# Ones rows, v cast and row halves placed anew at the start of an attention and feed-forward kernel

## The chip, the cores and the metric

The kernel runs on one NeuronCore of a Trainium2 chip. The metric is the device time of one execution in microseconds. The core has TensorE (PE, with PEld for its weight loads), VectorE (DVE), ScalarE (ACT), GpSimd (POOL) and SyncE (SP), which here only issues DMAs. Each engine works through its own queue in order.

## The reference

Attention with a mask from hash buckets (4 batches, 8 heads, 768 positions, head size 64), then a feed-forward layer of 2048 on the 3072 rows of 512:

```python
q_bucket = sum((q @ proj > 0) * 2 ** arange(6))       # k_bucket likewise
scores = where(q_bucket == k_bucket, q @ k.T / 8, -1e9)
attn = softmax(scores)                                # minus the row maximum
x = (attn @ v) as 3072 x 512
h = x @ w_in
g = where(h >= 1, h, where(h <= -1, 0, (h + 1) ** 2 / 4))
out = g @ w_out
```

## The kernel before

The 32 heads go two by two, as 16 pairs. Every fp32 operand is split into a high part that TensorE takes and a low rest. For a pair, T2 holds the high parts with some extra rows and T1 the low ones. Rows 0 to 7 of T2 carry the hash bits, scaled so that unequal buckets push the score far down. For the first pair the row maximum is in row 32 of T2[0]: in `T2[0][32:33, 0, h]` lies the clamped maximum of each query (the max row), and in `T2[0][32:33, 1, h]` lie ones that it is multiplied with (the ones row). For later pairs the max row is row 7.

A head is cut into 12 units (NU) of 128 keys by 384 queries. In the main loop step g does, on TensorE, the score matmuls of unit g (`s_unit`, lines 350 and 351), the three value matmuls of unit g - 4 (`pv_unit`, lines 383 to 385), and in some steps one of the six pairs of maxima matmuls of a later head (`max_mm`, line 310), whose result VectorE reduces in the next step (`max_red`, line 314). All maxima share one PSUM tile, `smax`. ScalarE takes the exponential twice for each unit, VectorE or POOL subtracts to get the low part (`lo_unit`, line 39; POOL for units 0 and 3 of each six). Other work is put into steps by `at(g, function, ...)`; within a step it is recorded behind the unit's own work, in the order of the calls. `early` says in which steps the maxima of heads 0 to 4 lie; from then on every second step has one.

Ahead of the loop the first pair is prepared by hand. `prep_first(0)` on VectorE and `prep_first(1)` on POOL split the raw tiles, `place_first` issues DMAs that put rows in place, `first_mm` computes the projections, `first_cmp` and `first_scale` make bits of them, and `max_first` computes the maxima of the first three query blocks of head 0 in six matmuls with a filler each (`keep_busy`, line 402). The other three blocks of head 0 come in steps 0 to 2, those of head 1 in steps 3 to 8. `row_clamp` clamps maxima into a helper tile, `row_mm` transposes them by small matmuls (line 254), and ScalarE copies the row into T2[0] (`row_half`, `row_both`). `quarter` splits a quarter of the second pair, `move` copies parts between T1 and T2, `bits_mm`, `bits_cmp`, `bits_scale` and `bits_put` make the bits rows of a later pair, `load_v`, `cast_v` and `split_v` bring v, `weights_pair` makes the split projection for two heads.

The order on each engine is that of the recorded calls. What an instruction waits for follows from the tiles that it reads and writes: a matmul that reads rows 0 to 127 of `T2[0][:, 1, h]` waits for the last recorded write to any of these rows.

Of the kernel before, what the change touches and what calls it, by code (L numbers as in the profile page):

```python
# [11 lines left out]
F32 = mybir.dt.float32  # L12
# [9 lines left out]
NB = 6  # L22
# [91 lines left out]
def attention(ctx, tc, wst, T1, T2, qk, v, pj, cv, x_d, s_d, e_d, tasks, shared):  # L114
# [16 lines left out]
    nrow = [const.tile([P, NJ, 33], F32R, name=f"nrow{h}") for h in range(2)]  # L131
    pj_raw = const.tile([P, NB], F32, name="pj_raw")
    pj_hi = const.tile([P, NB], F32R, name="pj_hi")
    pw = const.tile([P, 3, P], F32R, name="pw")
# [8 lines left out]
    def load_raw(pr):  # L143
        raws[pr] = work.tile([P, 2, S], F32, name="raw", bufs=1)
        nc.sync.dma_start(out=raws[pr], in_=qk[pr])

# [10 lines left out]
    def move(pr, part):  # L157
        t1, t2 = T1[pr % NQK].bitcast(F32), T2[pr % NQK].bitcast(F32)
        src, dst = ((t2[0:64, 1], t2[64:128, 0]), (t2[64:128, 1], t1[0:64, 1]),
                    (t1[64:128, 0], t1[64:128, 1]), (t2[0:64, 1], t1[64:128, 0]))[part]  # L160
        nc.sync.dma_start(out=dst, in_=src)
# [4 lines left out]
    def prep_first(h, raw, eng):  # L166
# [16 lines left out]
        if h == 1:  # L183
            for sl in halves:
                low(sl)

    def place_first(h):
# [60 lines left out]
    def row_flags(hd):  # L248
        nc.vector.tensor_scalar(out=nms[hd][:, NJ:2 * NJ], in0=nms[hd][:, 0:NJ], scalar1=CLAMP, scalar2=None,
                                op0=ALU.is_gt)  # L250
# [5 lines left out]

    def row_both(hd):
        ps = ps_m.tile([P, 2, 512], F32, name="smax")
        for hf in range(2):
            row_mm(hd, hf, ps[:, hf])  # L260
        nc.scalar.copy(out=T2[0][32:33, 0, hd, :].rearrange("p (f n) -> p f n", f=2), in_=ps[32:33, :, 0:HS])

    def row_half(hd, hf):
        ps = obank[hf]
        row_mm(hd, hf, ps)
        nc.scalar.copy(out=T2[0][32:33, 0, hd, hf * HS:(hf + 1) * HS], in_=ps[32:33, 0:HS])
# [49 lines left out]

    mx = {}

    def max_clamp(hd, eng):
# [79 lines left out]

    def keep_busy():  # L400

        nc.tensor.matmul(out=scratch[:, 0:2 * P], lhsT=idle[:, 0:P], rhs=idle, start=True, stop=True)

    def weights_pair(part):

        if part == 0:
            nc.scalar.copy(out=pj_hi, in_=pj_raw)
        for i, r, c in ((0, 0, 0), (0, 64, 16), (1, 0, 8), (1, 64, 24)):
            rows = slice(r, r + 64)
            if part == 0:  # L410
                nc.scalar.copy(out=pw[rows, i, c:c + NB], in_=pj_hi[rows].bitcast(F32))
            else:
                sub(nc, nc.gpsimd, pw[rows, i, 32 + c:32 + c + NB], pj_raw[rows], pj_hi[rows].bitcast(F32))
# [35 lines left out]
    nc.vector.memset(T2[0][0:64, 0].bitcast(F32), 0.0)  # L449
    for _ in range(12):  # L450
        keep_busy()
# [6 lines left out]
    for t in PH:  # L458
        nc.gpsimd.memset(t[:, HS:HS + 2].bitcast(F32), 1.0)
    for r, c in ((0, 0), (64, 32)):  # L460
        nc.scalar.copy(out=pw[r:r + 64, 2, c:c + NB], in_=pj_raw[r:r + 64])
    prep_first(0, first[0][:, 0], nc.vector)
    place_first(0)
    load_raw(1)
    load_v(0)
    for hf in range(2):
        first_mm(0, hf, obank[hf])
    nc.gpsimd.memset(T2[0][32:33, 1, 0].bitcast(F32), 1.0)
    for _ in range(5):
# [13 lines left out]
    for hf in range(2):  # L483
        first_mm(1, hf, ps_s.tile([P, 512], F32, name="s"))
    row_half(0, 0)
    for hf in range(2):
        first_cmp(1, hf)
    for _ in range(4):
        keep_busy()
    for t in VB:  # L490
        nc.gpsimd.memset(t[:, :, 1].bitcast(F32), 0.0)
    for t in PL:
        nc.gpsimd.memset(t[:, HS:HS + 2].bitcast(F32), 0.0)

    def quarter(n):
# [7 lines left out]

    quarter(0)
    quarter(1)
    at(0, first_scale, 1, 1, nc.vector)
    at(1, cast_v, 0, nc.vector)
    for h in range(2):
        at(1, split_v, 0, nc.gpsimd, h)
    at(1, weights_pair, 0)  # L510
    at(2, first_scale, 1, 0, nc.vector)
    at(9, lambda: nc.vector.memset(T2[0][32:33, 1, 1].bitcast(F32), 1.0))
    for n in (2, 3):
        at(n, quarter, n)
    at(2, weights_pair, 1)
    at(10, load_v, 1)
    at(3, row_clamp, 0, NJ // 2, NJ)
    at(5, load_raw, 2)
    at(4, row_half, 0, 1)
    for n in range(3):  # L520
        at(4, move, 1, n)
    for hf, n in enumerate((5, 7)):
        at(n, bits_mm, 1, hf, 1)
        at(n + 1, bits_cmp, 1, hf)
    at(5, row_flags, 0)
    at(6, lambda: nc.gpsimd.memset(T2[1][0:64, 0].bitcast(F32), 0.0))
    at(11, max_tr, 0, 0)
    at(11, max_put, 0)
    at(9, row_clamp, 1, 0, NJ)
    at(8, move, 1, 3)  # L530
    at(8, bits_scale, 1, nc.scalar)
    at(9, bits_put, 1)
    at(10, row_both, 1)
    at(11, row_flags, 1)
    at(12, lambda: nc.gpsimd.memset(T2[2][0:64, 0].bitcast(F32), 0.0))
    at(15, max_tr, 1, 0)
    at(15, max_put, 1)
    at(2 * NU + 1, lambda: nc.gpsimd.memset(T2[0][32:33, 0].bitcast(F32), 0.0))
    for hd in range(NH):
        pr, h = hd // 2, hd % 2  # L540
        g = hd * NU
        if hd + 2 < NH:
            gc, gt = ((NU + 8, NU + 8), (2 * NU + 4, 2 * NU + 6))[hd] if hd < 2 else (g + NU, g + NU + 4)
            at(gc, max_clamp, hd + 2, nc.gpsimd if hd > 1 else nc.vector)
            at(gt, max_tr, hd + 2, 1)
            at(gt + (hd > 1), max_put, hd + 2)
        if h == 0 and pr + 2 < NPAIR:
            g0 = g + (9 if pr == 0 else 0)
            for n in range(4):
# [5 lines left out]
            if pr + 3 < NPAIR:  # L555
                at(g0 + 7, load_raw, pr + 3)
            bits_at = ((7, 1), (11, 0)) if pr else ((13, 0), (17, 1))
            for hf, (n, bank) in enumerate(bits_at):
# [3 lines left out]
            at(g + n + 2, bits_scale, pr + 2, nc.gpsimd)  # L562
            at(g + (18 if pr else 21), bits_put, pr + 2)
        if h == 0 and pr + 1 < NPAIR:
            gv = g + LAG + (2 if pr else 10)
            at(gv, cast_v, pr + 1, nc.scalar)
            at(gv + 1, split_v, pr + 1, nc.gpsimd, 0)
            at(gv + 3, split_v, pr + 1, nc.gpsimd, 1)
            if pr + 2 < NPAIR:
                at(gv + 6, load_v, pr + 2)  # L570

    NG = NH * NU
    red = None
    early = {n: (0, NJ // 2 + n) for n in range(NJ // 2)}
    for hd, gs in ((1, range(3, 9)), (2, range(14, 20)), (3, (20, 21, 23, 24, 26, 27)),
                   (4, (28, 29, 31, 32, 34, 35))):
        early.update({n: (hd, i) for i, n in enumerate(gs)})
    for g in range(NG + LAG + 1):
# [5 lines left out]
        if 1 <= g <= NG:  # L584
            lo_unit(g - 1)
        if g < 3 * NU:
            due = g in early
            hd, i = early.get(g, (0, 0))
        else:
            hd, i = g // NU + 2, (g % NU) // 2  # L590
            due = hd < NH and g % 2 == 0
# [661 lines left out]
```

## Time and profile before

| | us |
|---|---|
| median of 3 runs | 985.62 (983.16 to 987.43) |
| the profiled execution | 986.29 |
| its span | 984.5 |
| PE busy | 968.2 |
| DVE busy | 799.5 |
| ACT busy | 679.3 |
| POOL busy | 342.1 |

The span is what the trace covers; the execution's own time is 1.8 us longer. Granted clock means TensorE's clock as a share of full speed; its mean over the span was 0.996. In the views, a row of the timeline is start, duration, engine, line, operation, output and input, with the idle time just before it and what ended it in brackets.

### The profile page before, as it was taken

The page shows a single profiled execution, that of the slowest core. Times are in us where ns is not written, and L with a number is a line of the kernel's source. Part 1 is how long each engine was busy: PE and PEld are TensorE (multiplying, and loading weights), DVE is VectorE, ACT ScalarE, POOL GpSimd, SP SyncE. Part 2 cuts the span into 40 slices and gives each one's busy share as a digit, 9 for nine tenths or more (in the row PEclk, how much of TensorE's full clock was granted, in tenths as well). Part 3 has the DMA queues.
Part 4 walks back from the last instruction along what each step waited for, and adds up shares of the span by engine and source line. Part 5 has one row for each costly group of instructions (what it writes and reads, how often), then busy time and mean ns, then how long its engine had stood idle before and what let it go on. Part 6 is the DMA issues. An engine that isn't in the chain of part 4 may idle for free.

```text
span 984.5 us, 15564 instructions
## 1 busy us (share of the span) xinstructions
PE 968.2 (98%) x5047; PEld 891.9 (91%) x5047; DVE 799.5 (81%) x1359; ACT 679.3 (69%) x1483; POOL 342.1 (35%) x411
## 2 busy tenths in 40 slices
PE   7999999999999999999999999999999999999998
PEld 5789999999999999999999998888988888988896
DVE  8789999999999999988798887887876777655554
ACT  6779888998999888988655556555564545554444
POOL 7666777778877777766100000000000000000000
PEclk8999999999999999999999999999999999999999
DMA  6654667766656667554496478977449554454431
GB/s 174 177 154 101 174 179 191 199 173 168 177 140 180 173 187 191 136 146 124 127 286 217 118 245 271 299 239 210 118 151 245 147 185 116 130 168 118 115 93 64
DMA packets 94712, 167.55 MB, mean 170 GB/s; under 512 B 13940, under 2 KB 51432, under 8 KB 94632
## 3 DMA queue, kind: packets, MB, share of 16 engines
q1 hardware_dynamic: 94408, 166.56, 59.3%
q8 instruction: 40, 0.66, 0.3%
q14 instruction: 40, 0.33, 0.1%
q10 hardware_dynamic: 224, 0.00, 0.0%
HBM read 106.13 MB, written 33.87 MB: 142 GB/s over the span
## 4 chain that ended last, share of the span: by engine, by line
PE 90%; DVE 5%; ACT 2%; DMA 1%; issue 1%; SPq 0%; DVEq 0%
PE y L791 27%; PE h L1023 18%; PE smax L310 7%; PE h L928 7%; PE o L385 6%; PE s L351 6%; PE o L384 6%; PE o L383 6%; PE s L350 6%; PE o L204 2%; DVE nm L314 2%; DMA vraw<-in_v_dram 1%; DVE pl L39 1%; DMA t<-te 1%; ACT ph L359 0%
## 5 line engine op out<-in xcount | busy, mean ns | idle before, releaser
L359 ACT ACTIVATE ph<-s 128x384 fp32r<-128x384 f32 x380 | 188.1, 495 | 47.5 <-PE s L351 41.8
L314 DVE TENSOR_REDUCE nm<-smax 128x1 f32<-128x768 f32 x189 | 178.9, 947 | 16.2 <-PE smax L310 14.5
L39 POOL TENSOR_TENSOR pl<-pf,ph 128x384 fp32r<-128x384 f32 x128 | 139.0, 1089 | 90.4 <-ACT pf L364 90.1
L756 DVE SCALAR_TENSOR_TENSOR t<-t 128x384 f32<-128x384 f32 x128 | 71.3, 557 | 101.7 <-ACT z L751 101.5
L39 DVE TENSOR_TENSOR pl<-s,ph 128x384 fp32r<-128x384 f32 x256 | 135.5, 544 | 10.2 <-ACT s L364 9.4
L350 PE MATMUL s<-t 128*128 128x384 f32 x384 | 132.6, 345 | 0.0
L385 PE MATMUL o<-pl,va 128*128 128x386 f32 x384 | 130.6, 340 | 0.4 <-DVE pl L39 0.4
L384 PE MATMUL o<-ph,vb 128*128 128x386 f32 x384 | 130.6, 340 | 0.0
L351 PE MATMUL s<-t 128*128 128x384 f32 x384 | 130.3, 339 | 0.2 <-DMA t<-te 0.2
L383 PE MATMUL o<-ph,va 128*128 128x386 f32 x384 | 130.2, 339 | 0.1
L364 ACT ACTIVATE s<-s 128x384 f32<-128x384 f32 x252 | 124.9, 496 | 0.0
L791 PE MATMUL y<-t,ghi 128*128 128x512 f32 x384 | 124.6, 395 | 0.0
L310 PE MATMUL smax<-t 128*128 128x384 f32 x378 | 104.0, 356 | 6.6 <-DVE nm L314 6.1
L750 ACT ACTIVATE t<-h,mh 128x384 f32<-128x384 f32 x56 | 32.6, 581 | 84.4 <-PE h L928 44.3
L310 PEld LDWEIGHTS smax<-t 128*128 128x128 f32 x378 | 65.5, 191 | 23.5 <-DVE nm L314 23.0
L761 ACT CAST ghi<-z 128x384 fp32r<-128x384 f32 x129 | 65.1, 505 | 30.1 <-DVE z L757 26.3
L751 ACT ACTIVATE z<-t,m 128x384 f32<-128x384 f32 x128 | 79.0, 617 | 4.2
L1023 PE MATMUL h<-wbig,t 128*128 128x384 f32 x399 | 81.4, 336 | 0.0
L791 PEld LDWEIGHTS y<-t,ghi 128*128 128x128 f32 x384 | 71.3, 188 | 11.1 <-ACT ghi L761 0.3
L1023 PEld LDWEIGHTS h<-wbig,t 128*128 128x128 f32 x399 | 71.6, 188 | 5.3
L791 PE MATMUL y<-t,glo 128*128 128x512 f32 x192 | 76.0, 396 | 0.0
L791 PE MATMUL y<-woh,glo 128*128 128x512 f32 x192 | 75.7, 394 | 0.2
(181 smaller groups left out, 2092.0 us busy)
## 6 DMA issues: line engine op xcount, KB each, us to landing
t<-wc SPq DMA_DIRECT2D x92, 256.0 KB
t<-t SPq DMA_DIRECT2D x60, 384.0 KB
wraw<-wc SPq DMA_DIRECT2D x76, 256.0 KB
raw<-in_qk_dram SPq DMA_DIRECT2D x15, 768.0 KB
wraw<-in_w_in_dram SPq DMA_DIRECT2D x16, 512.0 KB
wraw<-in_w_out_dram SPq DMA_DIRECT2D x16, 512.0 KB
t<-ed SPq DMA_DIRECT2D x36, 192.0 KB
xd<-xs SPq DMA_DIRECT2D x32, 192.5 KB
```

The source lines that it names most:

```text
L39: eng.tensor_tensor(out=out, in0=a, in1=b, op=ALU.subtract)
L310: nc.tensor.matmul(out=smax[hd][:, hf, 0:HS], lhsT=t2[:, 0, h, i * P:(i + 1) * P], rhs=t2[:, 1, h, hf * HS:(hf + 1) * HS], start=True, sto ...
L314: nc.vector.tensor_reduce(out=nmp(hd)[:, i:i + 1], in_=smax[hd][:, :, 0:HS], axis=AX.XY, op=ALU.max, negate=True)
L350: nc.tensor.matmul(out=ps[:, 0:HS], lhsT=t1[:, 1, h, ks], rhs=t1[:, 0, h, sl], start=True, stop=False)
L351: nc.tensor.matmul(out=ps[:, 0:HS], lhsT=t2[:, 1, h, ks], rhs=t2[:, 0, h, sl], start=False, stop=True)
L359: nc.scalar.activation(out=ph[:, 0:HS], in_=ps[:, 0:HS], func=AF.Exp, scale=SCALE)
L364: nc.scalar.activation(out=pf, in_=ps[:, 0:HS], func=AF.Exp, scale=SCALE)
L383: nc.tensor.matmul(out=o, lhsT=wa, rhs=ph, start=(jj == 0), stop=False)
L384: nc.tensor.matmul(out=o, lhsT=wb, rhs=ph, start=False, stop=False)
L385: nc.tensor.matmul(out=o, lhsT=wa, rhs=pl, start=False, stop=(jj == NJ - 1))
L791: nc.tensor.matmul(out=ys[c][m], lhsT=g_[:, m * P:(m + 1) * P], rhs=w, start=(first and k == 0), stop=(last and k == 2))
L1023: nc.tensor.matmul(out=ps, lhsT=w[:, cs], rhs=x, start=(n == 0 and s not in (2, 3, 6)), stop=(n == 5), skip_group_check=True)
```

## The change

- v of the first pair is loaded ahead of the second pair's raw tile, which comes in two halves. The v cast goes from VectorE to POOL, ahead of the loop, with the split of its first head; the split of the second head is put in step 10.
- The pair weights are made on POOL, before and inside the second head's preparation. The first head's ones row is set behind that on POOL, the second head's in step 2 on POOL (before: step 9 on VectorE).
- `first_scale` of the second head and `row_flags` go to POOL.
- The fourth pair of maxima of head 0 comes ahead of the loop, the others in steps 0 and 2, those of head 1 in steps 4 to 12.
- The second head's max row is set in two halves, steps 7 to 9 and 13 to 14. The third head's maxima are clamped, transposed and put in two halves, steps 18 to 25.
- The quarters, moves, bits and v of the second and third pair are put in other steps; the raw load of the third pair goes out ahead of the bits rows and of later moves.
- From head 5 on, maxima lie two steps later, their clamps one.
- Two more fillers at the start; the four behind the first row write into another bank.

```diff
 def load_raw(pr):
-        nc.sync.dma_start(out=raws[pr], in_=qk[pr])
+        for sl in (slice(0, HS), slice(HS, S)) if pr == 1 else (slice(0, S),):
+            nc.sync.dma_start(out=raws[pr][:, :, sl], in_=qk[pr][:, :, sl])
...
 (prep_first, h == 1)
                 low(sl)
+            weights_pair(1)
+            ones_row(0)
+
+    def ones_row(h):
+        nc.gpsimd.memset(T2[0][32:33, 1, h].bitcast(F32), 1.0)
...
+    def half_clamp(hd, hf):
+        nm = nms[hd]
+        x = nm[:, hf * HB:(hf + 1) * HB]
+        nc.vector.tensor_scalar(out=nmh[:, hf, HB:2 * HB], in0=x, scalar1=CLAMP, scalar2=None, op0=ALU.is_gt)
+        nc.vector.tensor_scalar(out=nmh[:, hf, 0:HB], in0=x, scalar1=CLAMP, scalar2=None, op0=ALU.min)
+
+    def half_put(hd, hf, bank):
...
+        nc.tensor.transpose(out=ps[0:2 * HB, 0:P], in_=nmh[:, hf], identity=ident)
+        te = small.tile([2 * NJ, P], F32R, name="te")[0:2 * HB]
+        nc.scalar.copy(out=te, in_=ps[0:2 * HB, 0:P])
...
-    for _ in range(12):
+    for _ in range(14):
         keep_busy()
...
+    weights_pair(0)
...
-    load_raw(1)
     load_v(0)
+    load_raw(1)
...
-    nc.gpsimd.memset(T2[0][32:33, 1, 0].bitcast(F32), 1.0)
...
-    row_half(0, 0)
+    for n in (0, 1):
+        max_mm(0, NJ + n)
+    row_half(0, 0, 0)
+    max_red(0, NJ // 2)
     for hf in range(2):
         first_cmp(1, hf)
     for _ in range(4):
-        keep_busy()
+        keep_busy(obank[1])
+    cast_v(0, nc.gpsimd)
...
+    split_v(0, nc.gpsimd, 0)
...
-    quarter(0)
-    quarter(1)
-    at(0, first_scale, 1, 1, nc.vector)
-    at(1, cast_v, 0, nc.vector)
...
-    at(9, lambda: nc.vector.memset(T2[0][32:33, 1, 1].bitcast(F32), 1.0))
...
-    at(5, load_raw, 2)
...
+    for t in (1, 0):
+        at(0, first_scale, 1, t, nc.gpsimd)
+    at(2, ones_row, 1)
     at(3, row_clamp, 0, NJ // 2, NJ)
+    at(4, row_half, 0, 1, 1)
+    for n, g in enumerate((1, 4, 5, 6)):
+        at(g, quarter, n)
...
+    at(7, row_clamp, 1, 0, NJ // 2)
...
+    at(9, row_half, 1, 0)
...
+    at(10, load_raw, 2)
...
+    at(13, row_clamp, 1, NJ // 2, NJ)
+    at(14, row_half, 1, 1, 0)
...
-    early = {n: (0, NJ // 2 + n) for n in range(NJ // 2)}
-    for hd, gs in ((1, range(3, 9)), (2, range(14, 20)), (3, (20, 21, 23, 24, 26, 27)),
-                   (4, (28, 29, 31, 32, 34, 35))):
+    early = {}
+    for hd, gs in ((0, (0, 2)), (1, (4, 5, 6, 8, 11, 12)), (2, (15, 16, 17, 19, 20, 22)),
+                   (3, (21, 23, 24, 26, 27, 29)), (4, (30, 31, 33, 34, 36, 37))):
...
-            hd, i = g // NU + 2, (g % NU) // 2
+            hd, i = (g - 2) // NU + 2, (g - 2) % NU // 2
```

How the rows move on the engines. First POOL's queue from its last memset of the tiles ph on, before the loop; t_0_77 is T2[0], t_2_76 the first pair's low rest, raw tiles of the first pair are wraw. Before:

```order
L459 MEMSET ph_160 128x2
L468 MEMSET t_0_77 1x768
L175 CAST t_0_77<-wraw 128x384 x2
L39 TENSOR_TENSOR t_2_76<-wraw,t_0_77 128x384 x2
L491 MEMSET vb_152 128x6x64
```

After:

```order
L481 MEMSET ph_161 128x2
L429 CAST pj_hi<-pj_raw 128x6
L433 CAST pw<-pj_hi 64x6 x4
L177 CAST t_0_77<-wraw 128x384 x2
L39 TENSOR_TENSOR t_2_76<-wraw,t_0_77 128x384 x2
L39 TENSOR_TENSOR pw<-pj_raw,pj_hi 64x6 x4
L192 MEMSET t_0_77 1x768
L290 CAST va_151<-vraw 128x6x2x64
```

The memset of the first head's ones row (1x768) went from the first place to behind the weights and the second head's preparation.

Then the same queue in the loop's first steps, from the last memset of the tiles pl on; t_1_78 and t_1_75 are T2 and T1 of the second pair, pl low parts of the units, vb the low part of v. Before:

```order
L493 MEMSET pl_167 128x2
L150 CAST t_1_78<-raw 128x384
L39 TENSOR_TENSOR t_1_75<-raw,t_1_78 128x384
L39 TENSOR_TENSOR pl_161<-pf,ph_154 128x384
L39 TENSOR_TENSOR vb_152<-vraw,va_150 128x6x64 x2
```

After:

```order
L519 MEMSET pl_168 128x2
L39 TENSOR_TENSOR vb_153<-vraw,va_151 128x6x64
L248 TENSOR_SCALAR t_0_77<-xs,cvd 8x768 x2
L39 TENSOR_TENSOR pl_162<-pf,ph_155 128x384
L152 CAST t_1_78<-raw 128x384
L39 TENSOR_TENSOR t_1_75<-raw,t_1_78 128x384
L192 MEMSET t_0_77 1x768
```

The second head's bits (L248) and its ones row (the last memset) are now in this queue, with one low part and one quarter between them.

Last TensorE, from the first score matmuls to the first maxima of the second head; s are scores, smax maxima, o the value sums. Before:

```order
L350 MATMUL s<-t_0_74 128x384
L351 MATMUL s<-t_0_77 128x384
L310 MATMUL smax<-t_0_77 128x384 x2
L350 MATMUL s<-t_0_74 128x384
L351 MATMUL s<-t_0_77 128x384
L310 MATMUL smax<-t_0_77 128x384 x2
L350 MATMUL s<-t_0_74 128x384
L351 MATMUL s<-t_0_77 128x384
L310 MATMUL smax<-t_0_77 128x384 x2
L350 MATMUL s<-t_0_74 128x384
L351 MATMUL s<-t_0_77 128x384
L310 MATMUL smax<-t_0_77 128x384 x2
```

After, the last rows ahead of the second head's first maxima, from step 3 on:

```order
L372 MATMUL s<-t_0_74 128x384
L373 MATMUL s<-t_0_77 128x384
L372 MATMUL s<-t_0_74 128x384
L373 MATMUL s<-t_0_77 128x384
L405 MATMUL o_137<-ph_156,va_151 128x386
L406 MATMUL o_137<-ph_156,vb_153 128x386
L407 MATMUL o_137<-pl_163,va_151 128x386
L311 MATMUL smax<-t_0_77 128x384 x2
L261 MATMUL o_138<-ident_r,nrow_145 33x128 x3
```

The second head's first maxima came in step 3 right behind those of the first head; now they come in step 4 behind five score units and the first value unit, and read the ones row that POOL sets.

98 lines of the change are left out of this document (50 added, 48 removed).

## The prediction

> **What bounds the kernel now.** I read the page first, then stage windows, then the waits of the engine that is busiest, then its neighbours at the places where it waits.
>
> ```profile
> span 984.5 us, 15564 instructions
> PE 90%; DVE 5%; ACT 2%; DMA 1%; issue 1%; SPq 0%; DVEq 0%
> ```
>
> The profiled execution took 986.29 us, 1.8 us more than its span; the three timed runs have a median of 985.62, so 0.67 us less. All sums below start from 986.29. TensorE carries 90% of the chain that ended last, so the question is where TensorE stands still or runs slowly. The windows (busy us with counts for PE, PEld, DVE, ACT, POOL, then granted clock, DMA share, GB/s) answer that:
>
> ```profile
> 5.00:6.30 1.30, 1.15 (x8) 0.85 (x7) 1.00 (x3) 0.87 (x2) 0.73 (x1) 1.00 0.03 9
> 14.80:18.20 3.40, 1.01 (x5) 0.65 (x4) 2.92 (x5) 2.08 (x7) 3.32 (x5) 0.99 0.47 123
> 18.20:21.60 3.40, 2.60 (x8) 2.60 (x9) 2.69 (x4) 1.72 (x5) 3.21 (x6) 0.50 0.42 89
> 21.60:25.00 3.40, 3.40 (x14) 3.25 (x13) 2.71 (x4) 1.34 (x3) 3.30 (x4) 0.50 0.85 202
> 25.00:38.40 13.40, 11.88 (x70) 11.19 (x70) 10.13 (x17) 10.37 (x24) 8.39 (x11) 1.00 0.54 142
> 38.40:80.00 41.60, 39.54 (x212) 35.79 (x212) 33.61 (x51) 31.27 (x75) 25.61 (x29) 1.00 0.61 163
> 80.00:600.00 520.00, 518.49 (x2812) 489.98 (x2811) 476.62 (x748) 425.10 (x983) 289.71 (x325) 1.00 0.62 174
> 600.00:984.50 384.50, 380.41 (x1880) 339.86 (x1879) 259.06 (x509) 196.38 (x367) 0.00 (x0) 1.00 0.56 166
> ```
>
> From 80 us to 600 us TensorE is idle for 1.5 us of 520. Nothing that the change does there can bring more than that. The reachable time lies ahead of 38.4 us, in idle TensorE and in the 6.8 us from 18.2 to 25.0 at a granted clock of 0.50, where 6.0 busy us cost 3.0 us more than at full clock. TensorE's timeline names the waits:
>
> ```profile
> 5.72 0.76 PE L402 MATMUL smax<-idle 128*128 128x256 f32 x5
> 7.23 0.41 PE L422 MATMUL s<-t 128*128 128x384 f32 x1 [0.76 <-ACT t L239]
> 13.86 0.62 PE L310 MATMUL smax<-t 128*128 128x384 f32 x2 [0.70 <-DVE nm L314]
> 16.77 0.62 PE L310 MATMUL smax<-t 128*128 128x384 f32 x2 [1.93 <-DVE nm L314]
> 19.00 1.01 PE L310 MATMUL smax<-t 128*128 128x384 f32 x2 [1.26 <-DVE nm L314]
> 33.65 0.52 PE L254 MATMUL smax<-ident_r,nrow 128*33 128x128 f32 x6 [1.36 <-DVE nrow L245]
> 38.23 0.34 PE L385 MATMUL o<-pl,va 128*128 128x386 f32 x1
> 38.41 0.51 PE L310 MATMUL smax<-t 128*128 128x384 f32 x2
> 38.75 0.34 PE L350 MATMUL s<-t 128*128 128x384 f32 x1
> ```
>
> The three waits between 13 and 19 us come from VectorE, which itself stood behind the v load:
>
> ```profile
> 10.86 0.17 DVE L245 TENSOR_SCALAR nrow<-nm 128x3 fp32r<-128x3 f32 x1
> 11.11 1.01 DVE L232 TENSOR_TENSOR xs<-s,xs 40x384 f32<-40x384 f32 x2
> 12.85 0.96 DVE L314 TENSOR_REDUCE nm<-smax 128x1 f32<-128x768 f32 x1
> 15.29 0.56 DVE L289 CAST va<-vraw 128x768 fp32r<-128x768 f32 x1 [1.48 <-DMA vraw<-in_v_dram]
> 19.34 0.59 DVE L245 TENSOR_SCALAR nrow<-nm 128x3 fp32r<-128x3 f32 x1
> ```
>
> **What the change takes away.** The v cast leaves VectorE, and with it the 1.48 us stall; the waits of 1.93 and 1.26 us and, if the clock then holds, its 3.0 us go. The second head's rows are set in halves, the first half eight units earlier than its last maxima, so the 1.36 us wait at 33.65 goes. The ceiling of all this, with nothing put in its place, is 1.93 + 1.26 + 1.36 + 3.0 = 7.6 us. But all that was taken off VectorE and ScalarE is now in POOL's queue ahead of two small memsets that TensorE waits for.
>
> **First term: the first ones row.** The memset of row 32 used to be the first thing POOL did for the first head; it now stands behind the pair weights and all of the second head's preparation. The first head's maxima read that row's tile, so TensorE's first one waits for it. POOL's prices:
>
> ```profile
> 3.43 0.41 ACT L461 CAST pw<-pj_raw 64x6 fp32r<-64x6 f32 x2 [0.78 <-DMA pj_raw<-in_pj_dram]
> 5.53 0.73 POOL L468 MEMSET t<- 1x768 f32 x1 [2.52 <-DVE t L39]
> 6.33 1.08 POOL L175 CAST t<-wraw 128x384 fp32r<-128x384 f32 x2
> 7.38 1.98 POOL L39 TENSOR_TENSOR t<-wraw,t 128x384 fp32r<-128x384 f32 x2
> 9.30 0.77 POOL L491 MEMSET vb<- 128x384 f32 x2
> 10.02 0.29 POOL L493 MEMSET pl<- 128x2 f32 x7
> 13.24 0.50 POOL L150 CAST t<-raw 128x384 fp32r<-128x384 f32 x1 [2.94 <-DMA raw<-in_qk_dram]
> 13.83 1.02 POOL L39 TENSOR_TENSOR t<-raw,t 128x384 fp32r<-128x384 f32 x1
> 17.63 2.27 POOL L39 TENSOR_TENSOR vb<-vraw,va 128x384 fp32r<-128x384 f32 x2
> 20.82 0.99 POOL L39 TENSOR_TENSOR pw<-pj_raw,pj_hi 64x6 fp32r<-64x6 f32 x4
> 47.14 0.98 POOL L273 TENSOR_SCALAR bits<-neg,cvt 32x768 fp32r<-32x768 f32 x1
> ```
>
> The projection lands at 3.43. The five small casts on POOL are not in the trace; the nearest row is the four 64x6 subtractions in 0.99, so about 0.25 each and 1.3 in all, to 4.7 (nothing to 2.5 us as bounds, of which only what passes 5.0 counts). The second head's data are in by about 5.0, since the DMA share falls to 0.03 there. Then casts and subtractions 6.33 to 9.36 in before, 3.03; four weight subtractions 0.99; the memset 0.73; hand-overs 0.1. That is 5.0 + 3.03 + 0.99 + 0.73 + 0.1 = **9.85** where before had 7.23. Bounds: 9.6 if the casts start at 4.7, 11.2 if they start at 6.33 as before. TensorE has nothing from 6.48 (the five fillers end) to 9.85: 3.4 us idle, 2.6 more than now. The two further fillers at the start cost at most 0.1, since the second half of the first head's preparation on VectorE ends later anyway.
>
> **Second term: the second ones row.** Call 9.85 T. VectorE's six reductions and the clamp ended 3.80 after 7.23; the new clamp meets POOL's v split and, like the row at 19.34, lasts until POOL's instruction ends: T + 4.35 (3.80 without it). Then one reduction 0.95 and two compares 1.01: T + 6.3. Only now may POOL scale the second head's bits: two at 0.98 (row at 47.14, same length, more partitions), the first low part 1.02, a cast and its low part 1.6, the memset 0.73: T + 11.6, 21.5 us. POOL's work before that (v cast 1.0 at twice the row at 13.24, memsets 0.77 and 0.3, split 1.05) ends by T + 4.3 even if v lands at 11, so the v load, now first in the queue, is hidden; it could land as late as 13 before it showed.
>
> ```profile
> 11.49 0.47 ACT L266 CAST t<-o 1x384 fp32r<-1x384 f32 x1
> ```
>
> TensorE comes to the first maxima of the second head, which wait for that memset, with five score pairs (1.75, at the 0.18 pitch of the rows at 38.23), one value unit 0.53, two maxima pairs 0.70, a wait of 0.7 (it is ready for the next maxima at T + 6.55, the reduction behind the compares ends at T + 7.25), from a start at T + 5.2 (clamp, three small matmuls, ScalarE's row copy of 0.47): T + 8.9. It stands there for **2.7 us** (bounds 1.5 to 4). Behind it in TensorE's queue are the rows of the first head and all score units, and no other engine gets work meanwhile.
>
> **Third term: from there to pair 1's first maxima** (38.41 in before). 11 score units 3.85, 11 value units 5.8, six maxima pairs 2.1, eight bits matmuls 1.4, nine row matmuls 0.6, waits for reductions in adjacent units 0.3: 14.1, to 35.6. At that point after has done one unit more (0.88) and four bits matmuls less (0.70). Gain: 38.4 - 35.6 + 0.2 = **3.0 us**, at full clock. The bits rows leave ScalarE near T + 22.9, two DMA issues of 0.8 follow (row below), and TensorE needs them at T + 25.8: no wait by about 1 us, if a small DMA lands within 1.3 us; a loss of up to 1.5 if not. The third pair's load now goes out as soon as POOL has read the raw tile, T + 16.1, instead of behind two more moves; TensorE needs its casts 10 us later, so 2.5 us later than before costs nothing.
>
> ```profile
> 23.44 0.58 SPq L145 DMA_DIRECT2D raw<-in_qk_dram  x1
> 31.73 3.27 SPq L282 DMA_DIRECT2D t<-bits  x4
> ```
>
> **The rest**: rows of the third head in halves add one 6-row transpose, one ScalarE copy and two DMAs, beside a busy TensorE, 0.1 us. Later maxima two units on, clamps one unit on: the transposes keep their units, work is equal, and 80 to 600 us has only 1.5 us idle; I take 0, bounds -1 and +1. Flags on POOL instead of VectorE: 0, POOL has idle time after 25 us.
>
> **Fourth term: the clock.** Before, the 3.4 us from 14.8 with 1.01 us busy were followed by 6.8 us at 0.50. The new schedule has two emptier places: 3.4 us idle before T, 2.7 us before 21.5. If the stretches lie as in before (18.2 to 21.6), TensorE is busy there for 0.6 us, and the next 3.4 us, all busy, run at half: 1.7 us lost. The first gap at half clock would cost about 0.85, since VectorE's reductions bound what follows. I take one stretch, 1.7.
>
> Sum: 986.3 - 3.0 + 1.7 = **985.0 us**; against the median 985.6, 0.1% less.
>
> The Trainium skill bears on two rows. "SBUF — State Buffer", section "SBUF: two separate sides", says that VectorE in some modes and GpSimd lock one port pair for a whole instruction. The clamp agrees (0.17 alone, 0.59 to within 0.03 us of the end of POOL's split); without the lock everything behind the clamp would come 0.55 earlier, 984.5. It speaks against moving work to POOL.
>
> **Rivals.** (a) *The clock holds* through both gaps: 986.3 - 3.0 = 983.3. For it: 2.7 us is shorter than the 3.4 us stretches in which the clock changed. Against: 1.01 busy us in such a stretch was not enough. The Trainium skill's "TensorE: Matmul & The Clock Gate", section "Part 1: The HAM clock gate", has the half rate follow at least one idle window of about 3.4 us, which would give this case; the trace lost the clock after a stretch that was not idle. Chance 0.22.
> (b) *The ones rows don't gate*, because POOL's small instructions are quicker or come earlier than I set them: the stalls of 2.6 and 2.7 are not paid and the change does what it seems to be for: 986.3 - 3.0 - 5.3 = 978; half of it 980.6. Against: the memset of 1x768 has its row, and the order is the program's. Chance 0.14.
> (c) *POOL's queue becomes the bound and the result is slower*: place, the wait before the second head's first maxima. Without a drop in clock the gain is gone once the second ones row ends after 24.5 instead of 21.5 us; with the clock at half twice, once for the 6.8 us of before (3.4) and once for 0.85, it is gone already at 21.5: 986.3 - 3.0 + 4.25 = 987.5, and with the bits rows late by 1.5 and T at its late bound (1.35 more) 990.4. Chance 0.19.
> (d) The forecast, gains and stalls about equal: 985.0, 983.5 to 987. Chance 0.45.
>
> **Numbers.** 0.5% is 4.9 us and about what a measurement of this kernel can tell from no change. Faster than 980.7: most of (b) with a little of (a), 0.16. Slower than 990.5: the end of (c), 0.08. Between, 0.76. The range 980.3 to 989.5 leaves out the lower part of (b) and the end of (c).
>
> **What would show it.** In the profile after: TensorE's first head maxima start at 9.6 to 11.2 with a wait for the POOL memset; the first maxima of the second head wait 1.5 to 4 us for the second memset; no VectorE wait for v; pair 1's first maxima at 35.6 to 37.5; a granted clock of 0.50 for 3.4 us somewhere before 30 us. A first start near 7.3 would prove the first term wrong; no wait at the second head's maxima the second; a clock of 1.00 throughout the fourth. After 80 us TensorE's idle time should stay under 3 us.

## Result, and the profile after

The changed kernel took 996.3 us (median; 994.3 to 997.14), the kernel before 985.79 us beside it: a ratio of 1.0106, 95% interval 1.0079 to 1.0133. It is 10.5 us slower, where 985.0 was forecast. The profiled execution took 996.68 us.

The page of the kernel after, its span and the part of its chain by engine:

```profile
span 994.9 us, 15585 instructions
PE 83%; DVE 6%; ACT 6%; issue 2%; DMA 1%; POOL 1%; SPq 0%; POOLq 0%; DVEq 0%; ACTq 0%
```

TensorE's share of the chain fell from 90 to 83%, and ScalarE's rose from 2 to 6%. TensorE's timeline (start, duration, then in brackets the wait ahead and who ended it) has both waits that were forecast, and two that were not; the two rows without a wait are used further down:

```profile
10.59 0.69 PE L444 MATMUL s<-t 128*128 128x384 f32 x1 [3.67 <-POOL t L192]
23.64 1.01 PE L311 MATMUL smax<-t 128*128 128x384 f32 x2 [2.86 <-POOL t L192]
26.48 0.63 PE L311 MATMUL smax<-t 128*128 128x384 f32 x2
40.40 0.54 PE L311 MATMUL smax<-t 128*128 128x384 f32 x2
65.96 0.59 PE L311 MATMUL smax<-t 128*128 128x384 f32 x2 [3.16 <-DMA t<-bits]
70.85 1.65 PE L211 MATMUL o<-t,pw 128*128 128x384 f32 x4 [2.09 <-ACT te L355]
```

The rows at 10.59 and 23.64 wait for the ones rows on POOL. The last two are a second place: the bits rows of the third pair come 3.16 us late, and then ScalarE does. The windows of the same trace (busy us of PE, PEld, DVE, ACT, POOL, then granted clock, DMA share, GB/s) show the second place, and the stage behind it:

```profile
60.00:70.00 10.00, 5.42 (x26) 4.21 (x25) 5.73 (x8) 3.60 (x8) 9.04 (x12) 0.88 0.36 98
70.00:80.00 10.00, 8.99 (x40) 8.66 (x41) 5.05 (x8) 6.19 (x16) 2.90 (x3) 0.77 0.67 221
80.00:600.00 520.00, 516.53 (x2811) 488.65 (x2810) 475.51 (x741) 425.20 (x986) 296.99 (x329) 1.00 0.62 172
```

From 60 to 70 us TensorE works for 5.42 us of 10, and from 70 to 80 at a mean clock of 0.77. From 80 to 600 us it is idle for 3.5 us, 2 more than before.

A marker that both kernels share, in the same order, shows where the time goes: the copy of each finished output block on ScalarE. The fourth and the fifth of them, in before and then in after:

```profile
58.03 0.49 ACT L391 COPY xs<-o 128x386 f32<-128x386 f32 x1
67.42 0.49 ACT L391 COPY xs<-o 128x384 f32<-128x384 f32 x1
```

```profile
59.30 0.49 ACT L413 COPY xs<-o 128x386 f32<-128x386 f32 x1
75.56 0.49 ACT L413 COPY xs<-o 128x384 f32<-128x384 f32 x1
```

After is 1.27 us behind at the fourth copy and 8.14 behind at the fifth: **6.9 us are lost between two neighbouring blocks**, one more before the sixth, and nearly nothing from there to the twelfth. The table holds the start of these copies less that of before, for all kernels of this study, with the median time and the ratio to the kernel before:

| kernel | 1st (32.32) | 4th (58.03) | 5th (67.42) | 6th (75.26) | 12th (116.16) | median us | ratio, 95% interval |
|---|---|---|---|---|---|---|---|
| after | +0.55 | +1.27 | +8.14 | +9.27 | +9.28 | 996.3 | 1.0106 (1.0079 to 1.0133) |
| e1 | -0.87 | -0.61 | +1.46 | +4.24 | +4.23 | 990.77 | 1.0050 (1.0028 to 1.0071) |
| e2 | -3.46 | -2.54 | +4.44 | +5.57 | +5.55 | 994.27 | 1.0084 (1.0069 to 1.0099) |
| e3 | -2.75 | -2.47 | +4.77 | +6.49 | +6.46 | 993.38 | 1.0074 (1.0050 to 1.0097) |
| e4 | -7.63 | -6.47 | -5.26 | -4.11 | -4.15 | 984.42 | 0.9985 (0.9976 to 0.9994) |
| e5 | -1.55 | +3.56 | +4.79 | +5.92 | +5.90 | 993.74 | 1.0079 (1.0061 to 1.0096) |
| e6 | -1.08 | -0.78 | +0.35 | +1.48 | +1.48 | 989.67 | 1.0035 (1.0022 to 1.0049) |
| e7 | -0.66 | -0.67 | -0.67 | -1.05 | -1.08 | 986.56 | 1.0004 (0.9995 to 1.0013) |
| e8 | -7.41 | -2.58 | -2.50 | -1.37 | -1.41 | 987.67 | 1.0013 (1.0001 to 1.0025) |
| e9 | -7.38 | -6.25 | -3.10 | -1.36 | -1.36 | 984.79 | 0.9990 (0.9981 to 0.9999) |
| e10 | -7.32 | -6.15 | -4.33 | -1.58 | -1.57 | 985.31 | 0.9992 (0.9983 to 1.0001) |

The columns come from one profiled execution each, the times from all runs. The medians of before beside these runs lie between 985.67 and 986.18, and where the intervals of two rows overlap, a difference of some 2 us between them is not clear of the noise. At the first copy after has done less side work than before (14 instead of 18 maxima matmuls and 4 instead of 8 bits matmuls; e4 likewise); from the fourth copy on the counts of each kind differ by two at most, so the fourth column compares better than the first.

e1 and e5 carry out the same instructions as after in the first 45 us, and still stand 1.4 and 2.1 us earlier at the first copy. The granted clock accounts for it: after is at half for 6.8 and then 3.4 us, e1 for 6.8 us at the first place only, e5 for 3.4 us there only.

### The chain behind the 6.9 us

SyncE's queue, POOL, VectorE and ScalarE in the trace of after, four views:

```profile
28.83 2.37 SPq L163 DMA_DIRECT2D t<-t  x2
31.31 0.53 SPq L147 DMA_DIRECT2D raw<-in_qk_dram  x1
51.47 0.59 SPq L147 DMA_DIRECT2D raw<-in_qk_dram  x1
62.92 2.75 SPq L283 DMA_DIRECT2D t<-bits  x4
65.71 0.45 SPq L287 DMA_DIRECT2D vraw<-in_v_dram  x1
```

```profile
28.85 1.02 POOL L39 TENSOR_TENSOR t<-raw,t 128x384 fp32r<-128x384 f32 x1 [0.72 <-PE smax L311]
57.81 0.51 POOL L152 CAST t<-raw 128x384 fp32r<-128x384 f32 x1 [3.50 <-DMA raw<-in_qk_dram]
61.92 0.97 POOL L274 TENSOR_SCALAR bits<-neg,cvt 32x768 fp32r<-32x768 f32 x1
```

```profile
55.66 0.54 DVE L222 TENSOR_TENSOR neg<-o,neg 32x384 f32<-32x384 f32 x1
```

```profile
69.02 0.83 ACT L290 CAST va<-vraw 128x768 fp32r<-128x768 f32 x1 [5.83 <-DMA vraw<-in_v_dram]
```

In before, SyncE's queue and POOL at the same work:

```profile
43.24 0.59 SPq L145 DMA_DIRECT2D raw<-in_qk_dram  x1
51.40 0.36 SPq L286 DMA_DIRECT2D vraw<-in_v_dram  x1
51.86 2.82 SPq L282 DMA_DIRECT2D t<-bits  x4
```

```profile
52.00 0.51 POOL L150 CAST t<-raw 128x384 fp32r<-128x384 f32 x1
```

Before scaled the third pair's bits at 47.14, ahead of the fourth pair's first cast (52.00). After has them the other way round: the change moves the bits from step 19 to step 25, past the cast in step 24. The cast waits 3.50 us for its load, and the scale stands behind it: 61.92, 14.8 us later than before. VectorE had its input ready at 56.20 (55.66 and 0.54 us), so 5.7 us of this are the queue: POOL stood until 57.81 for the load, then did 4.1 us of work that comes ahead of the scale (the cast, its low part, a unit's low part, a memset). The rest is the later step. The bits rows follow at 62.92, the third pair's v load behind them in SyncE's queue at 65.71 (before had it ahead of them), ScalarE stands 5.83 us ahead of its v cast, and behind that cast stands the copy `te` that TensorE waits for at 70.85. The load that POOL waits for goes out 8.2 us later than before (51.47 against 43.24). The one before it went out 7.9 us later (31.31 against 23.44), and the change moves both the casts of that one (steps 13 to 16 instead of 9 to 12) and the next load (step 20 instead of 16). The raw tile has one buffer, but that is not what held this load: POOL had read the tile by 46.3, and e5 below, with the load in step 17, sends it at 46.69.

### The profile page after: what moved, and what is told of

It is laid out like the page before. It is cut to its first block, busy times and chain, and to the rows that moved or that the text cites. A ratio compares the mean times of both kernels' runs of the same rounds, so it can differ in the third digit from the quotient of the medians.

```text
span 994.9 us, 15585 instructions
## 1 busy us (share of the span) xinstructions
PE 972.0 (98%) x5050; PEld 895.4 (90%) x5050; DVE 797.5 (80%) x1358; ACT 679.2 (68%) x1480; POOL 349.2 (35%) x420
## 4 chain that ended last, share of the span: by engine, by line
PE 83%; DVE 6%; ACT 6%; issue 2%; DMA 1%; POOL 1%; SPq 0%; POOLq 0%; DVEq 0%; ACTq 0%
PE y L821 26%; PE h L1053 18%; PE h L958 7%; PE smax L311 6%; PE s L372 5%; PE s L373 5%; PE o L405 5%; PE o L407 5%; PE o L406 5%; DVE nm L315 3%; PE o L211 1%; ACT ph L381 1%; ACT va L290 1%; ACT s L386 1%; DVE pl L39 1%
## 5 line engine op out<-in xcount | busy, mean ns | idle before, releaser
L39 POOL TENSOR_TENSOR pl<-pf,ph 128x384 fp32r<-128x384 f32 x128 | 133.3, 1046 | 96.8 <-ACT pf L386 96.0
```

The source lines that it names most:

```text
L39: eng.tensor_tensor(out=out, in0=a, in1=b, op=ALU.subtract)
```

## The experiments

Seven kernels were run to find the cause and to price its parts, three to see whether the loads themselves can be had earlier.

**e1: the order on POOL.** The bits scale of the third pair is put ahead of the fourth pair's cast, its rows one step earlier; nothing else.

```diff
-            at(g + n + 2, bits_scale, pr + 2, nc.gpsimd)
-            at(g + (18 if pr else 26), bits_put, pr + 2)
+            at(g + n + (2 if pr else 1), bits_scale, pr + 2, nc.gpsimd)
+            at(g + (18 if pr else 25), bits_put, pr + 2)
```

> The changed kernel, with only the third pair's bits scaled on POOL ahead of the fourth pair's first cast (step 24 instead of 25), where that cast waits for its raw load. Queue theory (POOL's queue stood behind the late raw load, the bits rows, v and ScalarE behind that): the 3.2 us wait for the bits rows, most of the 2.1 us wait at L211 and the clock loss near 70 us go: 8 us less than the changed kernel, about 988. Rival, the raw load itself is too late: TensorE still waits for the fourth pair's casts, less than 4 us gained, 992 or more.

It gained 5.5 us (the means differ by 5.1, with a 95% interval of 2.4 to 7.7). POOL, and a wait of TensorE (total, times, longest) in the first 120 us, in e1:

```profile
54.16 0.98 POOL L274 TENSOR_SCALAR bits<-neg,cvt 32x768 fp32r<-32x768 f32 x1 [2.12 <-DVE neg L222]
58.63 0.51 POOL L152 CAST t<-raw 128x384 fp32r<-128x384 f32 x1 [3.49 <-DMA raw<-in_qk_dram]
```

```profile
PE o L211 <- ACT te L355: 0.3, 1, 0.3
```

The scale now runs at 54.16, while the cast still waits 3.49 us for its load. The wait for the bits is gone and that behind ScalarE is 0.3. From the fourth copy to the sixth e1 loses 4.9 us, and e6, which is the same program there, 2.3, where after lost 8.0. So 3.2 and 5.7 us of the 8.0 come back in the traces. The order of these two POOL instructions is the largest single cause. That all 8 us would come back was too much; the rival, which gave it 4 us at most, is passed by the medians and not excluded by the interval. The cast is as late as in after, and what stands behind it on POOL still holds TensorE, which waits 0.52 and 0.98 us for low parts from there (61.26 and 68.40 in e1).

**e2 and e3: each ones row by itself.** e2 sets the second ones row on VectorE in step 9, as before did; e3 sets the first one on POOL ahead of the second head's preparation.

```diff
-    at(2, ones_row, 1)
+    at(9, lambda: nc.vector.memset(T2[0][32:33, 1, 1].bitcast(F32), 1.0))
```

```diff
             weights_pair(1)
-            ones_row(0)
...
     for hf in range(2):
         first_mm(0, hf, obank[hf])
+    ones_row(0)
```

> The changed kernel, with the second head's ones row set on VectorE in step 9 as before. Theory (the second head's first maxima wait for POOL's memset): the 2.9 us wait at 23.6 us goes, the clock may hold there; 3 us less, 993, or up to 4.5 less with the clock. Rival (the wait near 63 us is set by the DMAs and POOL alone and takes back what comes earlier): under 1 us less.

> The changed kernel, with the first head's ones row set on POOL ahead of the second head's preparation, as before. Theory: the first maxima start near 7.5 us instead of 10.6, the 3.7 us wait falls under 1, the clock stays at 1.00 through 17 us; 3 to 4 us less, 992 to 993.5. Rival (the second ones row then gates alone, since POOL's chain to it hangs on VectorE only in part): the wait at the second head's maxima grows and under 1.5 us is gained.

2.0 and 2.9 us gained by the medians of four runs each; the intervals of both overlap that of after, so neither size is clear of the noise. In each trace the wait that it aims at is gone. Waits of TensorE up to 120 us, e2 and then e3:

```profile
PE smax L311 <- DMA t<-bits: 3.2, 1, 3.2
PE o L211 <- ACT te L355: 2.2, 1, 2.2
```

```profile
PE smax L310 <- POOL t L191: 3.9, 1, 3.9
PE smax L310 <- DMA t<-bits: 3.1, 1, 3.1
```

In e3 the stall at the second head's maxima grows from 2.86 to 3.9: TensorE comes there sooner and waits for the same POOL queue. In both the wait for the bits stays at 3.1 to 3.2, and the table has 8.1 and 9.0 us lost between the fourth and sixth copies: this place doesn't depend on the ones rows.

**e4: all three repairs together.**

> All three: both ones rows as before and the third pair's bits ahead of the fourth pair's cast. If the three stalls and the two clock drops are the whole loss and add up, 8 + 3 + 3.5 us less than the changed kernel: 980 to 983, faster than before by 3 to 6 us. If something else in the change costs (the later maxima, the halves), it stays above 986.

984.42 us, 0.15% under the kernel before, with an interval that leaves out 1; the expectation had 980 to 983. Against after it is 11.9 us, where the three apart give 10.5. So the three account for the whole loss against before. The granted clock is 1.00 in every window of 10 us up to 80. What the change was able to bring shows in the table: 6.47 us at the fourth copy (7.63 at the first, with less side work done), of which 4.15 are left at the twelfth. What was left between 50 and 60 us, on ScalarE and on TensorE in e4:

```profile
57.26 0.83 ACT L289 CAST va<-vraw 128x768 fp32r<-128x768 f32 x1 [1.82 <-DMA vraw<-in_v_dram]
59.09 0.96 PE L210 MATMUL o<-t,pw 128*128 128x384 f32 x4 [1.13 <-ACT te L354]
```

The v load is still late, and TensorE still waits behind its cast.

**e5: the load itself.** After, with only the fourth pair's raw load in step 17 instead of 20.

```diff
-                at(g0 + 7, load_raw, pr + 3)
+                at(g0 + (7 if pr else 4), load_raw, pr + 3)
```

> The kernel after, with only the fourth pair's raw load put back from step 20 to step 17 of the first units (ahead of the third head's first rows in SyncE's queue). Theory (the late load is the root of the stall between 60 and 80 us: cast at 57.81, the bits scale behind it in POOL's queue at 61.92, then the bits DMA, the v load, the v cast, the bits matmuls): the cast starts near 54.5, the bits scale about 3.3 us earlier, the 3.2 us wait for the bits DMA goes, and the time is 990 to 993, 3 to 6 us below the kernel after. Rival (only the order of cast and scale on POOL matters, and the scale still stands behind the cast): less than 1.5 us gained, 995 or more.

2.6 us by the medians, between what the theory and the rival gave, and not clear of the noise. SyncE's queue, POOL and TensorE in e5:

```profile
46.69 0.87 SPq L147 DMA_DIRECT2D raw<-in_qk_dram  x1
49.52 7.75 SPq L163 DMA_DIRECT2D t<-t  x2
```

```profile
55.99 0.50 POOL L152 CAST t<-raw 128x384 fp32r<-128x384 f32 x1 [4.41 <-DMA raw<-in_qk_dram]
```

```profile
55.45 0.69 PE L373 MATMUL s<-t 128*128 128x384 f32 x1 [3.10 <-DMA t<-te]
```

The load went out 4.8 us earlier and was there only 1.8 earlier: it took 9.3 us from issue to cast instead of 6.3. The wait for the bits rows is replaced by one of 3.1 for the third head's first half rows (1.5 KB), which were issued right behind the load, at 47.66. The row of 7.75 us holds two moves of 384 KB: the first went out at 49.52, the second at 56.81, after SyncE had waited 6.6 us for a copy between the tiles to land. The bits are scaled at 60.08, 1.8 us earlier than in after; but this execution was 2.1 us ahead at the first copy already, by the clock, so none of that is due to the load. From the first copy to the twelfth it gains 1.3 us on after, and the 2.6 us of the medians stay unexplained. The windows of 46 to 52 us, after and then before, and for before an earlier one:

```profile
46.00:52.00 6.00, 5.75 (x32) 4.93 (x31) 4.69 (x9) 3.72 (x9) 1.88 (x3) 1.00 0.96 259
```

```profile
46.00:52.00 6.00, 5.43 (x30) 4.49 (x29) 4.88 (x8) 3.98 (x11) 2.94 (x4) 1.00 0.62 185
40.00:50.00 10.00, 9.17 (x46) 7.50 (x47) 7.97 (x13) 6.19 (x16) 5.28 (x6) 1.00 0.91 237
```

The transfer engines are busy for 0.96 of this stretch in after, 0.62 in before. Before has a full stretch too, but earlier: 0.91 from 40 to 50 us, and its own load lies in it and is there when POOL comes to it (52.00, no wait). In after the second pair's v load (44.56), the outputs (45.18), the third pair's moves (47.10 and 50.91) and the fourth pair's load (51.47) follow each other where the bits and rows are due. That an earlier issue only shares engines that are full is argued from these shares; what e5 shows is that the load took longer and that the rows behind it came late.

**e6: the price of the clock at the first gap.** e1, with 37 instead of 5 idle matmuls there, so that TensorE doesn't stand still before the first maxima.

> The run with the bits scale ahead of the fourth pair's cast (990.8 us), with 37 instead of 5 idle matmuls ahead of the first head's first maxima, so that TensorE works through the gap of 3.7 us before 10.6. Their results are not used. Theory 1 (the granted clock falls because of that gap, and the half rate behind it costs something): the clock stays at 1.00 from 8 to 21 us and the time is 989 to 990, 1 to 2 us less. Theory 2 (VectorE's reductions bound what follows the gap, so the half rate there is free): the clock stays and the time is within 0.7 us of 990.8. Theory 3 (the clock falls anyway at the second gap): half rate somewhere from 21 to 28 us.

989.67 us, 1.1 less than e1 by the medians, which the scatter of e1 (989.24 to 994.46) covers. Windows of e1, then of e6:

```profile
10.00:20.00 10.00, 9.00 (x41) 8.37 (x42) 7.54 (x14) 5.73 (x12) 5.10 (x14) 0.73 0.59 173
20.00:30.00 10.00, 6.94 (x39) 5.97 (x38) 6.42 (x11) 6.07 (x15) 9.26 (x12) 1.00 0.17 38
```

```profile
10.00:20.00 10.00, 8.18 (x46) 6.47 (x44) 7.92 (x16) 5.90 (x14) 6.61 (x16) 1.00 0.59 179
20.00:30.00 10.00, 8.00 (x37) 7.53 (x38) 5.57 (x8) 4.80 (x12) 7.99 (x9) 0.83 0.20 42
```

The clock held at the first gap and fell at the second, which it had not done in e1. The second head's first two maxima pairs in e1, then in e6:

```profile
23.38 0.61 PE L311 MATMUL smax<-t 128*128 128x384 f32 x2 [2.89 <-POOL t L192]
25.05 0.62 PE L311 MATMUL smax<-t 128*128 128x384 f32 x2
```

```profile
21.84 0.96 PE L311 MATMUL smax<-t 128*128 128x384 f32 x2 [2.76 <-POOL t L192]
24.62 0.85 PE L311 MATMUL smax<-t 128*128 128x384 f32 x2
```

With the clock held, the second stall ends 1.5 us earlier, from first maxima that start at the same time (10.57 and 10.53): the half rate behind the first gap is not free, and theory 2 falls. At half clock the next pair comes 2.8 us later instead of 1.7, which gives 1.1 back, and at the first copy 0.2 us is left. Theory 3 held as well: the drop moved to the second gap. So theory 1 has its cause right, but its 1 to 2 us at the end are not shown: in the profiled executions the two differ by 2.75 us at the twelfth copy and by 0.2 at the fourth, behind which the two programs are the same.

**e7: the later maxima alone.** The kernel before, with only the last part of the change (maxima two units on, clamps one unit on, from the sixth head).

```diff
-            gc, gt = (...)[hd] if hd < 2 else (g + NU, g + NU + 4)
+            gc, gt = (...)[hd] if hd < 2 else (g + NU + 1 if hd > 2 else g + NU, g + NU + 4)
...
-        if g < 3 * NU:
+        if g < 3 * NU + 2:
...
-            hd, i = g // NU + 2, (g % NU) // 2
+            hd, i = (g - 2) // NU + 2, (g - 2) % NU // 2
```

> The kernel before, with only the last part of the change: from the fifth or sixth head on the maxima run two units later and the clamp one unit later; the first units are those of before. Theory (the later units cost nothing, all of the loss lies ahead of 85 us): the ratio to before is 0.999 to 1.001, and TensorE's idle time from 80 to 600 us stays within 1 us of the 1.5 of before. Rival (part of the loss is the later units, whose 17 waits for VectorE's maxima of 4.3 us in all stand in the trace of the kernel after): 2 us slower or more.

1.0004 (0.9995 to 1.0013): 0.4 us slower, 1.3 at most. The window of e7 has 3.0 us idle where before had 1.5, 0.5 more than the theory allowed:

```profile
80.00:600.00 520.00, 517.00 (x2808) 489.92 (x2808) 475.27 (x748) 424.16 (x980) 294.61 (x325) 1.00 0.63 174
```

So the later units cost about a microsecond at most, and the rest of the loss lies ahead of the sixth copy.

**e8, e9, e10: the loads earlier, on top of e4.** e8 issues both the fourth pair's raw load (step 17) and the third pair's v load (step 24) earlier; e9 only the v load, in step 24; e10 only the v load, in step 23.

```diff
-                at(g0 + 7, load_raw, pr + 3)
+                at(g0 + (7 if pr else 4), load_raw, pr + 3)
...
-                at(gv + 6, load_v, pr + 2)
+                at(gv + (6 if pr else 4), load_v, pr + 2)
```

> The run with all three repairs (984.4 us), with two loads put earlier in SyncE's queue as well: the fourth pair's raw load at step 17 instead of 20, and the third pair's v load at step 24, ahead of the bits rows of the third pair instead of behind them. Theory (the 2 us that TensorE still stands between 50 and 60 us, and the 1.1 us wait for ScalarE behind the v cast, come from these two late loads): both go, 982 to 983, 0.3 to 0.4% faster than before. Rival (the two loads only collide with the moves and rows that they now stand ahead of, and another wait takes their place): 984 to 986.

> The run with all three repairs (984.4 us), with only the third pair's v load moved, from step 26 to step 24: in SyncE's queue it stands ahead of the third head's second half rows and of the bits rows instead of behind them; the fourth pair's raw load stays at step 20. Theory (what is left between 50 and 60 us is ScalarE standing 1.82 us at the v cast with the row copy of the maxima behind it, and the run with both loads early lost because of the raw load alone): the v load goes out near 49.1 instead of 53.9, TensorE's wait of 1.1 us behind ScalarE goes, and the time is 982.5 to 983.7. Rival (any load ahead of the small rows costs what it brings, since the small transfers then wait for it): 984 to 986, with a wait for the bits rows or for the half rows.

> The same with the v load one step earlier still, at step 23, ahead of the third pair's last move, so that it goes out near 46.6 while the fourth pair's raw load (43.9 to 50.2) is under way. Theory (the transfer engines are full there, DMA share 0.91 from 40 to 50 us, so two loads at once only share them): the raw cast starts after 51.5 instead of 50.2, the last move lands later, and the time is 0 to 2 us above that of the v load at step 24. Rival (there is room): the raw cast within 0.5 us of 50.2 and a time equal or less.

None is under e4: 987.67, 984.79 and 985.31 against 984.42, and the theory of e8 and of e9 fell. Only e8 is slower than e4 beyond the noise; e9 and e10 can't be told from e4 or from each other. SyncE's queue, POOL and TensorE in e8:

```profile
41.48 1.01 SPq L147 DMA_DIRECT2D raw<-in_qk_dram  x1
44.06 8.99 SPq L163 DMA_DIRECT2D t<-t  x2
```

```profile
51.99 0.50 POOL L152 CAST t<-raw 128x384 fp32r<-128x384 f32 x1 [2.43 <-DMA raw<-in_qk_dram]
```

```profile
49.22 0.45 PE L372 MATMUL s<-t 128*128 128x384 f32 x1 [2.10 <-DMA t<-te]
```

The raw load, issued 2.4 us earlier than in e4 (43.87), is there 1.8 later (51.99 against 50.19): it goes out behind the second pair's v load (37.17) and two moves (39.74). TensorE waits 2.10 us for the third head's first half rows, issued behind the load at 42.59, and the mean clock from 50 to 60 us falls to 0.83. The row of 8.99 us is again two moves, 44.06 and 52.58, with 7.9 us of waiting for a copy between the tiles; the v load stands behind the second and so goes out at 53.15, hardly earlier than in e4 (53.86). TensorE and POOL in e9:

```profile
56.83 0.69 PE L372 MATMUL s<-t 128*128 128x384 f32 x1 [2.26 <-DMA t<-te]
```

```profile
53.06 0.50 POOL L152 CAST t<-raw 128x384 fp32r<-128x384 f32 x1 [3.41 <-DMA t<-bits]
```

The v load went out at 48.71 and the wait behind ScalarE fell from 1.13 to 0.3, as expected; in its place the third head's second half rows, issued behind the v load at 50.43, come 2.26 us late. In e10 the v load went out at 46.31 and the raw cast started at 52.84 instead of 50.19, as its theory said. But e9's raw cast is at 53.06 with the v load at 48.71, so one step more or less is not what delays it, and the 0.5 us between the two medians says nothing. In these four runs (e5, e8, e9, e10) whatever goes first between 40 and 55 us, another transfer goes late.

## Why the prediction was wrong

The profiled execution took 11.7 us more than the 985.0 forecast. By the copies 2.6 of these lie ahead of the fourth (+1.27 where 1.3 less than before was forecast), 8.0 between the fourth and the sixth, 1.1 behind the twelfth.

**First term (ones row at T = 9.85, bounds 9.6 to 11.2): right.** 10.59; the casts started at 5.85 rather than 5.0, behind their data.

**Second term (a stall of 2.7 us, bounds 1.5 to 4): right.** 2.86 us, at 23.6 rather than 21.5, since the first came 0.7 late and the clock was at half in between; in e6, with the clock held there, the wait is 2.76 and ends at 21.84. One step in it did not happen: the clamp was to last until POOL's split ended, for which the sum has 0.55 us, but it took 0.17 (at 14.84, when the split had ended at 14.15). A later clamp, at 20.91, did run beside POOL and took 0.40, to within 0.03 of the end of POOL's instruction. By the medians the removal of this wait brings 2.0 us (e2), that of the first 2.9 (e3), and both together 6.3 where the bits are mended (e4 against e1), which is clear of the noise.

**Third term (pair 1's first maxima at 35.6 to 37.5, a gain of 3.0): too early.** They started at 40.40 in after, and at 38.95 and 38.32 in e1 and e5 with the same instructions. The list of work from the second head's first maxima to there is right, instruction by instruction, but it takes 15.6 us in e1 and e5, at full clock, where the sum has 14.1. By the prediction's own count (0.2 us of work more in after) the three stand at +1.8, +0.3 and -0.3 us against before, where 3.0 gained and 1.7 lost make -1.3. The 1.36 us wait for the second head's row went as forecast, though its first half is put in step 9, three steps ahead of the last maxima (step 12), where the prediction has eight units.

**Fourth term (one stretch of 3.4 us at half, 1.7 us lost): mis-sized.** By windows of 1 us the clock in after was at half from 9.7 to 16.5, from 23.3 to 26.7, and again from 67.7 to 74.5. From the first maxima to the second head's it takes 11.3 us with the clock held (e6), 12.2 with 3.4 us at half (e5), 12.9 and 13.1 with 6.8 us at half (e1, after). So the first drop costs 0.9 us where it lasts 3.4 us, close to the 0.85 that the prediction names and leaves out of its sum, and 1.8 in after. The second is priced by after against e1: the wait is 2.9 us in both, only after's clock falls, and from 23.64 to 26.48 it needs 2.84 where e1 needs 1.67, so 1.2 us. Together 3.0 instead of 1.7. The third follows the wait for the bits; it is a result of the main loss.

**The rest (0.1 us, and 0 for 80 to 600 us): this is where the forecast failed.** Two things failed here. One is said at the end of the third term: the third pair's load goes out at T + 16.1, and "2.5 us later than before costs nothing". It went out at 31.31, 7.9 us later than before: POOL read the raw tile until 29.9, as its last parts are released by ScalarE and TensorE step by step (the row at 28.85 waits for TensorE), and two moves stand ahead of the load in SyncE's queue. What this costs by itself is not priced: e5, which sends the next load earlier, gains nothing clear of the noise. The other is what wasn't there: the sum stopped at 38.4 us and put the loss from 40 to 80 us at nothing, without a reason. The bits scale had been moved from step 19 to step 25, past a cast that waits for the next load, and the v load past the bits rows. The prediction followed POOL's queue through the second pair and not through the third and fourth. After loses 8.0 us there, from the fourth copy to the sixth; undoing one inversion (e1) gives back 5.5 by the medians.

**The later units: right.** e7 gives 0.4 us, interval -0.5 to 1.3. That the idle time after 80 us would stay under 3 us missed by 0.5.

**The rivals.** Rival (c) named POOL's queue as the bound, at the second head's first maxima, with 987.5 to 990.4. Up to the fourth copy that is what happened: the clock was at half twice there and after was 1.3 us behind before, where 987.5 is 1.2 above 986.3. That the numbers meet so closely is in part luck, since (c) priced the clock at 4.25 us and it cost 3.0, while the third term was 1.5 short. The larger loss came where POOL's queue became the bound again, at the third pair's bits. (a) and (b) fell: the clock dropped, and both ones rows gated.

What stays open: of the 6.5 us that e4 is ahead at the fourth copy 4.15 are left at the twelfth and 3.1 at the end of its span (981.4 against 984.5), 1.5 by the medians. The first part goes between 50 and 75 us, where four runs shifted transfers against each other, none of them with a gain clear of the noise; that fewer or spread transfers there would keep it was not tried. The last microsecond or so agrees with e7, but was not followed.

## What to carry to other kernels

When a change moves a step later, list what it is moved past on each in-order queue, and ask for each new pair whether the one now in front waits for something: here a scale of 0.97 us, put behind a cast that waited for a load, started 5.7 us after its input was ready, and putting it back in front brought 5.5 us by the medians. Carry the sum on until both kernels do the same work at the same distance again: this one stopped at 38 us, and the loss came at 65. Compare two kernels at a marker only where both have done the same work ahead of it. An earlier issue is not an earlier landing when other transfers are under way: 4.8 us at the issue were 1.8 us at the cast (e5).

## What the hardware showed that was not expected

The granted clock fell behind a wait of 2.86 us in after, and not behind one of 2.89 us in e1 and of 2.88 in e5, at the same instruction; after and e1 are 1.2 us apart by that alone. In after the clock fell 2.5 us after TensorE had stopped there (20.8 to 23.3), and at the first gap 2.8 us after (6.9 to 9.7). The Trainium skill, "TensorE: Matmul & The Clock Gate", section "Part 1: The HAM clock gate", lets the half rate follow at least one idle window of about 3.4 us; the wait in after was shorter than that, so here the trace differs. The half rate lasted 6.8, 3.4 and 6.8 us at the three places in after.

Small rows that are issued right behind a large load come late. In e5 the load, issued 4.8 us earlier, took 9.3 instead of 6.3 us, and TensorE waited until 55.45 for rows of 1.5 KB that were issued at 47.66. In e8 and e9 rows of the same size, issued at 42.59 and 50.43 behind such loads, were waited for until 49.22 and 56.83.
